# A threshold attention and FFN kernel: q and k transposed by TensorE instead of DMA, loads moved to SyncE, scores copied for the ACT path, weights loaded in pieces

## The chip, the cores and the metric

The kernel runs on one core of one Trainium2 chip. A core has five engines with a queue each, which run independently and wait for one another on semaphores: TensorE (PE; its weight loads are shown as PEld), VectorE (DVE), ScalarE (ACT), GpSimd (POOL) and SyncE (SP). SyncE computes nothing; it issues DMAs. DMAs issued by SyncE and by GpSimd run on the same 16 DMA engines. TensorE writes to PSUM, which DVE and ACT can read[...]; everything else is in SBUF.

The metric is the time of one execution on the device in microseconds, lower is better. Durations of single instructions come from one profiled execution.

## The reference

Eight batches of eight heads, 576 positions, head width 64. Attention keeps only the scores that lie within tau = 0.02 of their row's maximum:

```python
scores = scale * np.matmul(q, k.transpose(0, 1, 3, 2))        # scale = 1/8
thresh = np.max(scores, axis=-1, keepdims=True) - tau
scores = np.where(scores >= thresh, scores, -1000000000.0)
attn = np.exp(scores - np.max(scores, axis=-1, keepdims=True))
attn = attn / (np.sum(attn, axis=-1, keepdims=True) + 1e-09)
out = np.matmul(attn, v)
```

The attention output becomes x, of 4608 tokens by 512, and goes through a multiplicative FFN with d_ff = 1024:

```python
h = ((x @ w1) * (x @ w2)) @ w3
y = h @ w_out
```

Inputs and outputs are float32.

## The kernel before

**Pairs and units.** The work is cut into 32 pairs of heads (B = 8 batches, NP = 4 pairs each). A head's 576 rows are 512 main rows and 64 tail rows. The four main chunks of 128 rows of each of the two heads, and one chunk of the two tails together, give nine units (`UN`, L144). For a unit, `scores` (L147) multiplies q by k into a PSUM tile `S` of 128 x 576 floats; there are three such tiles.

**Precision.** A float32 value is carried as two bf16 numbers, a high part and the remainder. `hl` holds both side by side, 64 columns each, so that a transposed q chunk has the high parts on partitions 0 to 63 and the remainders on 64 to 127. Each score block takes two matmuls: against `kT`, and against `kB`, which is `kT` with its two partition halves swapped. So all four products of high parts and remainders are summed.

**Preparation.** `load_half` (L104) loads q, k and v of four heads, that is two pairs, with 13 DMAs that GpSimd issues. `prep_pair` (L123) then, for k and for q: DVE casts to the high part (L133), GpSimd subtracts for the remainder (L134), and SyncE issues a DMA transpose of the 128 x 1152 tile (L136). Two more SyncE DMAs build `kB` (L139, L140). ACT casts v (L127). The loop calls `load_half` two halves ahead and `prep_pair` two pairs ahead of use.

**Masking.** In `probs` (L174) a DVE pass over S finds the row's maximum less the margin (L188, the output `junk` is not used). Then a unit goes one of two ways, by the letter in `PATH` (L145). With A, ACT computes a leaky step from S (Prelu, L192) and an exponential of it with the row sum (L194). With P, ACT computes the exponential of S (L198) and DVE multiplies it by the mask and sums (L199). There are five P units and four A units per pair. The result `pm` of the two heads' chunks, 128 x 1152 bf16, is transposed by a DMA that SyncE issues (L203, four per pair; L206 for the tail unit). There are three `pm` tiles.

**Attention output.** `attend` (L210) takes the reciprocals of the row sums (L216), splits them on GpSimd (L218, L219), transposes them on PE (L224), spreads them over partitions with small matmuls (L230, L234), multiplies the transposed probabilities by v (L247, L259), and scales (L249, L260).

**FFN and the merged weight.** `merge_weights` multiplies w3 by w_out once into `wcb`, from DMA transposes of w3 (L90). `ffn` (L263) computes a batch's two products with w1 and w2 (L270), their product (L278), and the product with `wcb` (L286). `load_weights` issues four DMAs from GpSimd that cast to bf16 (L79 to L84).

**Order.** The main loop (L335) walks over 288 units. Generators on the `background` list are advanced by 0.72 steps per unit: first the weight loads, then the merge, then the FFN of finished batches. `attend` of a pair is written out as a block five units after the pair's last unit. The program order sets priorities; the framework's scheduler sets the final order within each engine's queue, and each queue runs in that order. Tiles with the same tag share their buffers, and a new tile waits until all uses of the one that it replaces have ended.

## Time and profile before

| | us |
|---|---|
| median of 3 runs | 683.06 (678.42 to 693.83) |
| the profiled execution | 677.28 |
| its span, first to last instruction | 675.3 |
| PE busy | 501.0 (74%) |
| PE weight loads busy | 260.1 (39%) |
| DVE busy | 456.4 (68%) |
| ACT busy | 388.0 (57%) |
| POOL busy | 241.0 (36%) |

The page of a profile gives busy times, the span in 40 equal slices with a digit for the busy tenths, the DMA queues with their packets and share of the 16 engines, the chain of work that ended last, the costliest groups of instructions, and the DMA issues. A group's line reads: source line, engine, operation, output <- inputs, shapes, count | busy us, mean ns of one | idle us of the engine before it, and what ended that idle time. A wait's line reads: who waited for whom, us in total, times, longest. A stretch's line gives for each engine its busy us and instructions, then the granted TensorE clock (1.00 is full), the DMA share and GB/s; a share can pass 1 because a packet's time includes its waiting. SPq is SyncE's queue. Matmuls overlap, so a busy PE is not PE at its peak.

### The profile page before, as it was taken

The page shows a single profiled execution, that of the slowest core. Times are in us where ns is not written, and L with a number is a line of the kernel's source. Part 1 is how long each engine was busy: PE and PEld are TensorE (multiplying, and loading weights), DVE is VectorE, ACT ScalarE, POOL GpSimd, SP SyncE. Part 2 cuts the span into 40 slices and gives each one's busy share as a digit, 9 for nine tenths or more (in the row PEclk, how much of TensorE's full clock was granted, in tenths as well). Part 3 has the DMA queues.
Part 4 walks back from the last instruction along what each step waited for, and adds up shares of the span by engine and source line. Part 5 has one row for each costly group of instructions (what it writes and reads, how often), then busy time and mean ns, then how long its engine had stood idle before and what let it go on. Part 6 is the DMA issues. An engine that isn't in the chain of part 4 may idle for free.

```text
span 675.3 us, 10319 instructions
## 1 busy us (share of the span) xinstructions
PE 501.0 (74%) x3163; PEld 260.1 (39%) x3208; DVE 456.4 (68%) x1181; ACT 388.0 (57%) x766; POOL 241.0 (36%) x378
## 2 busy tenths in 40 slices
PE   0530176658867888798878879888878888888996
PEld 0310042324434444344444435444434444444443
DVE  2630372259967898777968978798868988884231
ACT  1420162357756777566757766776766777774332
POOL 9870413513434344444343445344531120000000
PEclk9999988959979999777997979798998998999998
DMA  6999989889898999997899999999999988745011
GB/s 151 207 179 205 245 164 177 147 175 202 180 169 195 234 208 197 204 232 177 174 189 238 171 190 211 239 172 212 218 187 167 154 154 197 114 81 125 13 43 71
DMA packets 278566, 117.61 MB, mean 174 GB/s; under 512 B 261872, under 2 KB 262896, under 8 KB 277488
## 3 DMA queue, kind: packets, MB, share of 16 engines
q1 hardware_dynamic: 264112, 82.87, 67.7%
q0 software_dynamic: 14400, 34.09, 21.3%
q8 instruction: 25, 0.41, 0.3%
q14 instruction: 29, 0.24, 0.1%
HBM read 39.32 MB, written 9.44 MB: 72 GB/s over the span
## 4 chain that ended last, share of the span: by engine, by line
PE 42%; DMA 20%; DVE 12%; ACT 10%; issue 9%; POOL 4%; SPq 2%; DVEq 0%; POOLq 0%; ACTq 0%
PE ab L270 13%; PE S L157 9%; DMA pT<-pm 9%; PE av L247 7%; DVE junk L188 7%; PE yp L286 5%; DMA qT<-qhl 4%; ACT y L192 4%; PE S L162 2%; DMA kT<-khl 2%; DMA qf<-in_q_dram 2%; ACT pm L194 2%; DMA w3t<-w_223 2%; ACT bc L232 2%; PE tl L259 2%
## 5 line engine op out<-in xcount | busy, mean ns | idle before, releaser
L188 DVE TENSOR_SCALAR_CACHE_REDUCE junk<-S 128x576 bf16<-128x576 f32 x288 | 217.1, 754 | 33.0 <-PE S L157 17.3
L157 PE MATMUL S<-kT,qT 128*128 128x288 bf16 x512 | 148.3, 310 | 116.0 <-ACT y L192 60.3
L157 PEld LDWEIGHTS <-qT 128*128 128x128 bf16 x1024 | 99.6, 103 | 193.1 <-issue 94.8
L157 PE MATMUL S<-kB,qT 128*128 128x288 bf16 x512 | 148.1, 310 | 10.4 <-DMA kB<-kT 10.4
L192 ACT ACTIVATE y<-S,thr 128x576 bf16<-128x576 f32 x128 | 95.0, 742 | 99.3 <-DVE junk L188 97.7
L199 DVE SCALAR_TENSOR_TENSOR pm<-S,thr,e 128x576 bf16<-128x576 f32 x128 | 104.1, 813 | 42.2 <-DMA pT<-pm 41.7
L198 ACT ACTIVATE e<-S 128x576 f32<-128x576 f32 x160 | 102.7, 643 | 47.3 <-DVE junk L188 46.7
L194 ACT ACTIVATE pm<-y 128x576 bf16<-128x576 bf16 x128 | 87.2, 682 | 19.1 <-DMA pT<-pm 16.4
L134 POOL TENSOR_TENSOR khl<-kf,khl 128x576 bf16<-128x576 f32 x32 | 41.0, 1281 | 130.7 <-DVE khl L133 130.7
L278 DVE TENSOR_TENSOR ab<-ah,ab 128x512 bf16<-128x512 bf16 (+2 forms) x80 | 50.6, 633 | 52.3 <-PE ab L270 48.6
L275 ACT ACTIVATE ah<-ab 128x512 bf16<-128x512 f32 (+2 forms) x80 | 44.1, 552 | 51.0 <-PE ab L270 49.8
L286 PE MATMUL yp<-wcb,ab 128*128 128x512 bf16 (+1 forms) x280 | 71.9, 386 | 0.7 <-issue 0.2
L247 PE MATMUL av<-pT,vb 128*64 128x512 bf16 (+1 forms) x320 | 54.7, 458 | 20.1 <-ACT bc L232 13.0
L270 PE MATMUL ab<-xm,w2b 128*128 128x512 bf16 x250 | 66.6, 384 | 0.7 <-DVE ab L278 0.4
L270 PE MATMUL ab<-xm,w1b 128*128 128x512 bf16 x235 | 64.3, 380 | 0.8
L218 POOL CAST rhl<-rcp 128x9 bf16<-128x9 f32 x32 | 6.2, 193 | 161.0 <-DVE rcp L216 144.2
L133 DVE CAST khl<-kf 128x576 bf16<-128x576 f32 x32 | 23.8, 747 | 50.6 <-DMA kT<-khl 38.6
L134 POOL TENSOR_TENSOR qhl<-qf,qhl 128x576 bf16<-128x576 f32 x32 | 41.0, 1282 | 19.0 <-DVE qhl L133 18.7
L270 PEld LDWEIGHTS <-w2b 128*128 128x128 bf16 x320 | 29.0, 98 | 33.7 <-issue 11.7
L247 PEld LDWEIGHTS <-vb 128*64 128x64 bf16 (+1 forms) x320 | 21.1, 119 | 48.2 <-issue 42.6
L270 PEld LDWEIGHTS <-w1b 128*128 128x128 bf16 x320 | 28.4, 98 | 28.6 <-issue 2.7
L286 PEld LDWEIGHTS <-ab 128*128 128x128 bf16 (+1 forms) x296 | 28.0, 100 | 28.3 <-issue 1.8
(158 smaller groups left out, 625.4 us busy)
## 6 DMA issues: line engine op xcount, KB each, us to landing
kB<-kT SPq DMA_DIRECT2D x64, 144.0 KB, 2.7
kf<-in_k_dram POOLq DMA_DIRECT2D x32, 256.0 KB, 4.3
qf<-in_q_dram POOLq DMA_DIRECT2D x32, 256.0 KB, 5.4
vf<-in_v_dram POOLq DMA_DIRECT2D x32, 256.0 KB, 4.1
out_dram<-ys SPq DMA_DIRECT2D x8, 1024.0 KB, 5.1
pT<-pm SPq DMA_TRANSPOSE x128, 4.0
w_223<-in_moe_w_dram POOLq DMA_DIRECT2D x1, 2048.0 KB, 26.5
kf<-in_k_dram POOLq DMA_DIRECT2D x32, 32.0 KB, 4.3
```

Of the source, the lines that this page charges most:

```text
L134: nc.gpsimd.tensor_tensor(hl[:, :, 1, :], src[nm], hl[:, :, 0, :], ALU.subtract)
L157: nc.tensor.matmul(sp[:, half, 0:HB], lhsT=t["qT"][:, q0:q0 + 128], rhs=kk[w][:, c0:c0 + HB], start=(w == 0), stop=(w == 1))
L188: nc.vector.tensor_scalar(junk[:, :, :], sp, margin, -3e38, ALU.subtract, ALU.max, accum_out=thr[:, :])
L192: nc.scalar.activation(y[:, :, :], sp, AF.Prelu, scale=-1.0, bias=thr[:, :], alpha=0.125 / CUT)
L194: nc.scalar.activation(dst, y[:, :, :].rearrange("p a b -> p (a b)"), AF.Exp, scale=-CUT, accum_out=rs)
L198: nc.scalar.activation(e[:, :, :], sp, AF.Exp, scale=0.125)
L199: nc.vector.scalar_tensor_tensor(out=dst.rearrange("p (a b) -> p a b", a=2), in0=sp, scalar=thr[:, :], in1=e[:, :, :], op0=ALU.is_ge, op1= ...
L247: nc.tensor.matmul(av[o, :], lhsT=vb[kp, sl, :], rhs=pT[kp, :, sl, :], start=(g == 0), stop=(g == 4))
L270: nc.tensor.matmul(p[:, 0:nt], lhsT=w[:, c, f * 128:(f + 1) * 128], rhs=x(c), start=(c == 0), stop=(c == 3))
L275: nc.scalar.activation(ah[:, 0:nt], p[:, 0:nt], AF.Copy)
L278: nc.vector.tensor_tensor(ab[:, 0:nt], ah[:, 0:nt], ps[1][:, 0:nt], ALU.mult)
L286: nc.tensor.matmul(yp[0:c1 - c0, :], lhsT=abs_[f][:, c0:c1], rhs=wcb[:, f, :], start=(f == 0), stop=(f == NF - 1))
```

## The change

* q, k and v of four heads are loaded with one DMA each for the main rows, in runs of 1 KB, plus one each for the tail rows and one more for v. SyncE issues them, no longer GpSimd.
* The split of q and k into high part and remainder is done by GpSimd alone, and the cast of v too. Tails are split once per half, in `load_half`.
* TensorE transposes q and k, ten 128-column or 64-column pieces each, into a PSUM tile with the tag of the score tiles, and DVE copies it to SBUF. `kB` is built by two SyncE DMAs as before.
* `prep_pair` is now a generator with three steps, and runs one pair ahead: the split at unit 0, k's transposes at unit 5, q's at unit 7.
* In A units the DVE pass over S also writes the scores to SBUF, a small DVE instruction subtracts the margin from the maximum, and ACT's Prelu reads the SBUF copy. The tail unit becomes an A unit: four P and five A.
* `attend` is spread over the units of the next pair, a step at a time.
* The weights come in nine DMAs instead of four, one per background step, in program order on GpSimd's queue; w_out before w3.

```diff
--- before.py
+++ after.py
@@ -76,13 +76,21 @@
     wl = {}
 
     def load_weights():
-        nc.gpsimd.dma_start(w1b[:, :, :], moe_w1.rearrange("(c p) f -> p c f", p=128))
-        nc.gpsimd.dma_start(w2b[:, :, :], moe_w2.rearrange("(c p) f -> p c f", p=128))
+        def load(dst, src):
+            tc.keep_in_program_order(nc.gpsimd.dma_start(dst, src.rearrange("(c p) f -> p c f", p=128)))
+
+        for c in range(0, 4, 2):
+            load(w1b[:, c:c + 2, :], moe_w1[c * 128:(c + 2) * 128, :])
+            yield
+            load(w2b[:, c:c + 2, :], moe_w2[c * 128:(c + 2) * 128, :])
+            yield
         wl["w3"] = stage.tile([128, NF, d_ff], BF16, tag="w3", name="w3", bufs=1)
         wl["wo"] = stage.tile([128, NF, d_model], BF16, tag="wo", name="wo", bufs=1)
-        nc.gpsimd.dma_start(wl["w3"][:, :, :], moe_w3.rearrange("(c p) f -> p c f", p=128))
-        nc.gpsimd.dma_start(wl["wo"][:, :, :], moe_w_out.rearrange("(c p) f -> p c f", p=128))
-        yield
+        load(wl["wo"][:, :, :], moe_w_out)
+        yield
+        for c in range(0, NF, 2):
+            load(wl["w3"][:, c:c + 2, :], moe_w3[c * 128:(c + 2) * 128, :])
+            yield
 
     def merge_weights():
         for f in range(NF):
@@ -96,9 +104,7 @@
             yield
 
 
-
     pairs = {}
-
     halves = {}
 
     def load_half(m):
@@ -106,43 +112,66 @@
         b, h0 = divmod(4 * m, H)
         t = {}
         for nm, src in (("k", k), ("q", q), ("v", v)):
-            x = stage.tile([128, 2, 9, D], FP32, tag=nm + "f", name=nm + "f", bufs=2)
+            x = stage.tile([128, 4, 4, D], FP32, tag=nm + "f", name=nm + "f", bufs=2)
+            nc.sync.dma_start(
+                x[:, :, :, :].rearrange("p h j d -> p h (j d)"),
+                src[b, h0:h0 + 4, 0:M, :].rearrange("h (p j) d -> p h (j d)", j=4))
+            tails = src[b, h0:h0 + 4, M:S, :].rearrange("h r d -> r h d")
+
+            y = stage.tile([128 if nm == "v" else 64, 4, D], FP32, tag=nm + "t", name=nm + "t", bufs=2)
+            nc.sync.dma_start(y[0:64, :, :], tails)
+            if nm == "v":
+                nc.sync.dma_start(y[64:128, 0:2, :], tails[:, 1::2, :])
+            t[nm], t[nm + "t"] = x, y
+        for nm in ("k", "q"):
+            hl = stage.tile([64, 4, 2, D], BF16, tag=nm + "hlt", name=nm + "hlt", bufs=2)
+            nc.gpsimd.tensor_copy(hl[:, :, 0, :], t[nm + "t"][:, :, :])
+            nc.gpsimd.tensor_tensor(hl[:, :, 1, :], t[nm + "t"][:, :, :], hl[:, :, 0, :], ALU.subtract)
+            t[nm + "hlt"] = hl
+        vbt = stage.tile([128, 4, D], BF16, tag="vbt", name="vbt", bufs=3)
+        nc.gpsimd.tensor_copy(vbt[0:64, :, :], t["vt"][0:64, :, :])
+        nc.gpsimd.tensor_copy(vbt[64:128, 0:2, :], t["vt"][64:128, 0:2, :])
+        t["vbt"] = vbt
+        halves[m] = t
+
+    def prep_pair(n):
+
+        h = halves[n // 2]
+        h0 = 2 * (n % 2)
+        t = {"vbt": h["vbt"][0:64, h0:h0 + 2], "vbu": h["vbt"][64:128, n % 2]}
+        vb = stage.tile([128, 2, 4, D], BF16, tag="vb", name="vb", bufs=3)
+        nc.gpsimd.tensor_copy(vb[:, :, :, :], h["v"][:, h0:h0 + 2])
+        t["vb"] = vb
+        hls = {}
+        for nm in ("k", "q"):
+            hls[nm] = hl = stage.tile([128, 2, 4, 2, D], BF16, tag=nm + "hl", name=nm + "hl", bufs=2)
             for hh in range(2):
-                nc.gpsimd.dma_start(
-                    x[:, :, 5 * hh:5 * hh + 4, :].rearrange("p a j d -> p a (j d)"),
-                    src[b, h0 + hh:h0 + 4:2, 0:M, :].rearrange("h (p j) d -> p h (j d)", j=4))
-                nc.gpsimd.dma_start(
-                    x[64 * hh:64 * hh + 64, :, 4, :],
-                    src[b, h0 + hh:h0 + 4:2, M:S, :].rearrange("h r d -> r h d"))
-            t[nm] = x
-        x = stage.tile([64, 2, D], FP32, tag="v2f", name="v2f", bufs=2)
-        nc.gpsimd.dma_start(x[:, :, :], v[b, h0 + 1:h0 + 4:2, M:S, :].rearrange("h r d -> r h d"))
-        t["v2"] = x
-        halves[m] = t
-
-    def prep_pair(n):
-        src = {nm: x[:, n % 2] for nm, x in halves[n // 2].items()}
-        t = {}
-        vb = stage.tile([128, 9, D], BF16, tag="vb", name="vb", bufs=4)
-        nc.scalar.activation(vb[:, :, :], src["v"], AF.Copy)
-        vb2 = stage.tile([64, D], BF16, tag="vb2", name="vb2", bufs=4)
-        nc.gpsimd.tensor_copy(vb2[:, :], src["v2"])
-        t["vb"], t["vb2"] = vb, vb2
+                src = h[nm][:, h0 + hh, :, :]
+                nc.gpsimd.tensor_copy(hl[:, hh, :, 0, :], src)
+                nc.gpsimd.tensor_tensor(hl[:, hh, :, 1, :], src, hl[:, hh, :, 0, :], ALU.subtract)
+        pairs[n] = t
+        yield
         for nm in ("k", "q"):
-            hl = stage.tile([128, 9, 2, D], BF16, tag=nm + "hl", name=nm + "hl", bufs=2)
-            nc.vector.tensor_copy(hl[:, :, 0, :], src[nm])
-            nc.gpsimd.tensor_tensor(hl[:, :, 1, :], src[nm], hl[:, :, 0, :], ALU.subtract)
-            st = stage.tile([128, 9, 128], BF16, tag=nm + "T", name=nm + "T", bufs=3)
-            nc.sync.dma_start_transpose(st[:, :, :], hl[:, :, :, :].rearrange("p a b c -> p (a b c)"))
-            t[nm + "T"] = st[:, :, :].rearrange("p a b -> p (a b)")
-        kB = stage.tile([128, 9 * 128], BF16, tag="kB", name="kB", bufs=3)
-        nc.sync.dma_start(kB[0:64, :], t["kT"][64:128, :])
-        nc.sync.dma_start(kB[64:128, :], t["kT"][0:64, :])
-        t["kB"] = kB
-        pairs[n] = t
+            hl = hls[nm]
+            tp = psum.tile([128, 2048], BF16, tag="S", name="tp", bufs=3)
+            for hh in range(2):
+                nc.tensor.transpose(tp[:, M + hh * R:M + (hh + 1) * R], h[nm + "hlt"][:, h0 + hh, :, :],
+                                    ident[0:64, 0:64])
+                for j in range(4):
+                    c0 = hh * (M + 2 * R) + j * 128
+                    nc.tensor.transpose(tp[:, c0:c0 + 128], hl[:, hh, j, :, :], ident[:, :])
+            st = stage.tile([128, 2 * S], BF16, tag=nm + "T", name=nm + "T", bufs=2)
+            nc.vector.tensor_copy(st[:, :], tp[:, 0:2 * S])
+            t[nm + "T"] = st
+            if nm == "k":
+                kB = stage.tile([128, 2 * S], BF16, tag="kB", name="kB", bufs=2)
+                nc.sync.dma_start(kB[0:64, :], t["kT"][64:128, :])
+                nc.sync.dma_start(kB[64:128, :], t["kT"][0:64, :])
+                t["kB"] = kB
+            yield
 
     UN = [(hh, i) for i in range(4) for hh in range(2)] + [(2, 4)]
-    PATH = "PAPAPAPAP"
+    PATH = "PAPAPAPAA"
 
     def scores(n, u):
         t = pairs[n]
@@ -184,17 +213,22 @@
         dst = t["pm"][:, hh, :] if hh < 2 else pms[n % 2][:, 0:S]
         rs = t["rs"][:, u:u + 1]
         thr = work.tile([128, 1], FP32, tag="thr", name="thr", bufs=4)
-        junk = work.tile([128, 2, HB], BF16, tag="junk", name="junk", bufs=1)
-        nc.vector.tensor_scalar(junk[:, :, :], sp, margin, -3e38, ALU.subtract, ALU.max,
-                                accum_out=thr[:, :])
         if PATH[u] == "A":
-            y = work.tile([128, 2, HB], BF16, tag="y", name="y", bufs=2)
-            nc.scalar.activation(y[:, :, :], sp, AF.Prelu, scale=-1.0, bias=thr[:, :],
+
+            sc = work.tile([128, S], FP32, tag="sc", name="sc", bufs=3)
+            nc.vector.tensor_scalar(sc[:, :].rearrange("p (a b) -> p a b", a=2), sp, 1.0, -3e38,
+                                    ALU.mult, ALU.max, accum_out=thr[:, :])
+            y = work.tile([128, S], BF16, tag="y", name="y", bufs=2)
+            thm = work.tile([128, 1], FP32, tag="thm", name="thm", bufs=4)
+            nc.vector.tensor_scalar(thm[:, :], thr[:, :], margin, None, ALU.subtract)
+            nc.scalar.activation(y[:, :], sc[:, :], AF.Prelu, scale=-1.0, bias=thm[:, :],
                                  alpha=0.125 / CUT)
-            nc.scalar.activation(dst, y[:, :, :].rearrange("p a b -> p (a b)"), AF.Exp,
-                                 scale=-CUT, accum_out=rs)
+            nc.scalar.activation(dst, y[:, :], AF.Exp, scale=-CUT, accum_out=rs)
         else:
-            e = work.tile([128, 2, HB], FP32, tag="e", name="e", bufs=3)
+            junk = work.tile([128, 2, HB], BF16, tag="junk", name="junk", bufs=1)
+            nc.vector.tensor_scalar(junk[:, :, :], sp, margin, -3e38, ALU.subtract, ALU.max,
+                                    accum_out=thr[:, :])
+            e = work.tile([128, 2, HB], FP32, tag="e", name="e", bufs=2)
             nc.scalar.activation(e[:, :, :], sp, AF.Exp, scale=0.125)
             nc.vector.scalar_tensor_tensor(
                 out=dst.rearrange("p (a b) -> p a b", a=2), in0=sp, scalar=thr[:, :],
@@ -235,27 +269,25 @@
                              rhs=rTs[:, 64 * hh:64 * hh + 64], start=(hh == 0), stop=(hh == 1))
         nc.scalar.activation(bc[:, M:S], tl[:, 64:128], AF.Copy)
         yield
-        vb, vb2, pT, pTm = t["vb"], t["vb2"], t["pT"], t["pTm"]
+        vb, vbt, vbu, pT, pTm = t["vb"], t["vbt"], t["vbu"], t["pT"], t["pTm"]
         av = psum.tile([128, 512], FP32, tag="m", name="av")
         for g in range(5):
             for hh in range(2):
                 o = slice(64 * hh, 64 * hh + 64)
                 if g < 4:
-                    kp, sl = slice(0, 128), g + 5 * hh
+                    lhsT, rhs = vb[:, hh, g, :], pT[:, :, g + 5 * hh, :]
                 else:
-                    kp, sl = o, 4
-                nc.tensor.matmul(av[o, :], lhsT=vb[kp, sl, :], rhs=pT[kp, :, sl, :],
-                                 start=(g == 0), stop=(g == 4))
+                    lhsT, rhs = (vbu if hh else vbt[:, 0, :]), pT[o, :, 4, :]
+                nc.tensor.matmul(av[o, :], lhsT=lhsT, rhs=rhs, start=(g == 0), stop=(g == 4))
         nc.vector.tensor_tensor(xms[b][:, hp, :], av[:, :], bc[:, 0:M], ALU.mult)
         yield
         for g in range(5):
             for hh in range(2):
                 o = slice(64 * hh, 64 * hh + 64)
                 if g < 4:
-                    lhsT, rhs = vb[:, g + 5 * hh, :], pTm[:, g, o]
+                    lhsT, rhs = vb[:, hh, g, :], pTm[:, g, o]
                 else:
-                    lhsT = vb2[:, :] if hh else vb[0:64, 4, :]
-                    rhs = pTm[0:64, 4, o]
+                    lhsT, rhs = vbt[:, hh, :], pTm[0:64, 4, o]
                 nc.tensor.matmul(tl[o, 0:64], lhsT=lhsT, rhs=rhs, start=(g == 0), stop=(g == 4))
         nc.vector.tensor_tensor(xt[:, hp, b, :], tl[:, 0:64], bc[:, M:S], ALU.mult)
         yield
@@ -324,35 +356,43 @@
                 return
 
     load_half(0)
-    prep_pair(0)
+    for _ in prep_pair(0):
+        pass
     load_half(1)
-    prep_pair(1)
     background.append(load_weights())
     background.append(merge_weights())
     total = NPAIR * NU
-    LAG = 5
     credit = 0.0
-    for t in range(total + LAG):
+    running = []
+    prep = None
+    for t in range(total + NU):
         n, u = divmod(t, NU)
         if t < total:
             if u == 0 and n % 2 == 0 and n + 4 < NPAIR:
                 load_half(n // 2 + 2)
-            if u == 1 and n + 2 < NPAIR:
-                prep_pair(n + 2)
+            if u == 0 and n + 1 < NPAIR:
+                prep = prep_pair(n + 1)
+            if u in (0, 5, 7) and n + 1 < NPAIR:
+                next(prep)
             scores(n, u)
             probs(n, u)
-        d = t - LAG
-        if d >= 0 and d % NU == NU - 1:
-            m = d // NU
-            for _ in attend(m):
-                pass
-            if m % NP == NP - 1:
-                background.append(ffn_main(m // NP))
-                if m // NP == B - 2:
-                    background.append(ffn_tail(0, B - 1))
+        if running:
+            try:
+                next(running[0])
+            except StopIteration:
+                running.pop(0)
+                m = n - 1
+                if m % NP == NP - 1:
+                    background.append(ffn_main(m // NP))
+                    if m // NP == B - 2:
+                        background.append(ffn_tail(0, B - 1))
+        if u == 1 and n > 0:
+            running.append(attend(n - 1))
+            next(running[0])
         credit += 0.72
         step(int(credit))
         credit -= int(credit)
+    assert not running
     background.append(ffn_tail(B - 1, B))
     while background:
         step(1)
```

## The prediction

> **What bounds the kernel now.** I read the page's busy slices and DMA queues first, then the busy times by stretch, then landing times and waits, then single groups. From the page, one digit per fortieth of the span:
>
> ```profile
> PE   0530176658867888798878879888878888888996
> DVE  2630372259967898777968978798868988884231
> DMA  6999989889898999997899999999999988745011
> ...
> q1 hardware_dynamic: 264112, 82.87, 67.7%
> q0 software_dynamic: 14400, 34.09, 21.3%
> ```
>
> The DMA row is full from the second slice to about slice 33, whereas PE and DVE have holes in slices 3 to 8. q1 (SyncE's queue) is nearly all transposes. The stretches, each row giving busy us of PE, PEld, DVE, ACT, POOL, then granted clock, DMA share, GB/s:
>
> ```profile
> 0.00:21.60 21.60, 0.90 (x3) 0.28 (x3) 5.25 (x18) 2.54 (x3) 19.86 (x34) 1.00 0.72 181
> 47.00:80.00 33.00, 2.96 (x12) 1.39 (x10) 2.52 (x8) 3.57 (x7) 8.56 (x15) 1.00 1.14 219
> 80.00:143.00 63.00, 36.76 (x198) 18.12 (x200) 28.66 (x71) 23.86 (x45) 24.75 (x34) 0.83 0.99 176
> 143.00:509.00 366.00, 304.20 (x1985) 160.94 (x2013) 301.69 (x783) 251.70 (x499) 156.11 (x244) 0.92 1.01 198
> 509.00:615.00 106.00, 93.55 (x633) 49.49 (x642) 90.44 (x240) 78.65 (x157) 11.26 (x24) 0.97 0.75 140
> 615.00:675.30 60.30, 50.05 (x284) 23.23 (x287) 13.52 (x30) 16.89 (x35) 0.40 (x2) 0.97 0.21 60
> ```
>
> The reciprocal, one per head pair, marks progress: the first of the 32 starts at 47.1, the third at 143.3, the 25th at 509.0, the last at 615.1. So the kernel has four stages: 143.3 us for three pairs (start-up with weights), then 22 pairs at 16.6 us with loads, 7 at 15.2 us without, and 60 us of FFN remainder. In the third stage DVE has 13.7 us of work per pair, PE 13.8 and the DMA engines 1.01 x 16.6 = 16.8: DMA is the bound. In the fourth DMA is at 0.75 and the pace is still 15.2, 1.13 times PE's 13.4: that is the pace of the chain between engines. The start-up hole is DMA too. Landing times (last number, us) in 47 to 80, and the waits over the whole span (us, times, longest):
>
> ```profile
> kT<-khl SPq DMA_TRANSPOSE x1, 25.9
> qT<-qhl SPq DMA_TRANSPOSE x1, 21.3
> pT<-pm SPq DMA_TRANSPOSE x1, 10.5
> ```
>
> ```profile
> DVE pm L199 <- DMA pT<-pm: 41.7, 17, 5.8
> DVE khl L133 <- DMA kT<-khl: 38.6, 7, 24.3
> ```
>
> A transpose that lands in 4 us elsewhere takes 20 to 26 beside the weights, and DVE's cast waits 24 us at the head of its queue for the k buffer.
>
> **The change, part by part.**
>
> ```profile
> L188 DVE TENSOR_SCALAR_CACHE_REDUCE junk<-S 128x576 bf16<-128x576 f32 x288 | 217.1, 754 | 33.0 <-PE S L157 17.3 <-PE S L170 11.0
> L134 POOL TENSOR_TENSOR khl<-kf,khl 128x576 bf16<-128x576 f32 x32 | 41.0, 1281 | 130.7 <-DVE khl L133 130.7
> L218 POOL CAST rhl<-rcp 128x9 bf16<-128x9 f32 x32 | 6.2, 193 | 161.0 <-DVE rcp L216 144.2 <-PE S L157 16.7
> L133 DVE CAST khl<-kf 128x576 bf16<-128x576 f32 x32 | 23.8, 747 | 50.6 <-DMA kT<-khl 38.6 <-DMA kf<-in_k_dram 11.9
> L226 DVE COPY rTs<-rT 18x128 bf16<-18x128 bf16 x32 | 6.6, 207 | 2.1 <-PE rT L224 1.7
> L230 PE MATMUL bm<-rTs,sel 18*128 18x128 bf16 x128 | 13.8, 232 | 1.0 <-DVE rTs L226 1.0
> ```
>
> *DMA.* 64 transposes of q and k go. Each moves 1152 rows of 256 B, so 73,728 packets. q1's mean is 0.677 x 675.3 x 16 / 264,112 = 27.7 ns on one engine, so 73,728 x 27.7 / 16 = 128 us, 4.0 per pair. The loads move the same bytes from the same 1 KB runs, now on q1. I take their DMA time as unchanged: 12.8 us per pair are left, below PE and DVE. On SP, two transpose issues of about 1.36 us per pair become 3.5 load issues; an SP plain DMA takes 0.46 to 0.62 us here, about 2 us: no change. What is new is order: a load that waits for its buffer (free once GpSimd has split the half's second pair) holds the four P transposes behind it on SP, and ACT and DVE wait for P's buffers. Free if GpSimd is on time, up to 3 us every second pair if not.
>
> *GpSimd.* The 13 load issues per half (0.60 to 0.73 us each, 4.4 us per pair) and two subtractions (2.56) leave. From rows L134 and L218, a subtraction costs about 187 + 1.9 ns per element; the small casts (193 ns at 9 elements, 240 at 64) give 185 + 0.85. Per pair: v 0.62, four casts of 256 at 0.40, four subtractions at 0.67, tails 1.4, reciprocal 0.4: 6.7 us against 7.1 now. Here a rule speaks against the change: the Trainium skill, GPSIMD Engine Reference, "Engine selection", keeps two-input elementwise work off GpSimd as about twice as slow as VectorE. The row agrees on the ratio (1281 ns, against 576 elements at DVE's one per ns). By the rule the split would cost; by this trace GpSimd is idle over half of a pair, so 6.7 us is hidden unless its latency counts. k is needed at unit 5 (8 us in), q at unit 7 (11 us).
>
> *PE.* 20 transposes per pair. Four 128-column matmuls with their loads at L230 take 0.39 us, about 0.055 each after the first; so 20 cost 1.3 us with two group starts. The other end is 232 ns each without overlap, 4.6 us. I take 1.3, as they are independent. PE goes to 15.0 us per pair at the same clock. I know no reason for a gain.
>
> *DVE.* Out: two casts of 747 ns. In: two PSUM copies of 1152 bf16. At one element per cycle as L133 shows (about 1 ns, 150 fixed) a copy is 1.35 us. But L226 copies 128 elements from PSUM in 207 ns, when 150 + 133 would be 283; two per cycle give 217. By that row 0.75 us, equal to the casts. The Trainium skill, VectorE: DVE Perf Modes, "The perf-mode tier table", caps copies with PSUM at 2x, so it permits the row's value and no better. The fifth masked-multiply pass goes to ACT (-0.81 us); five threshold subtractions on one column enter, at most 207 ns each as for L226, at least 0.08 as the accumulator read: +0.65. DVE stays at 13.6 (14.8 at 1x). The maximum pass itself, with fp32 output, I keep at 754: its input from PSUM already runs one element per cycle.
>
> *ACT.* Minus v's cast (0.68 us), plus a Prelu, an Exp and an accumulator read (0.74 + 0.68 + 0.19) for an Exp of 0.64: +0.3, at 11.4 of 16 hidden. Reading SBUF copies frees a score buffer about one Prelu earlier (waits "S for ACT y" are 60 us in all), but two of eleven allocations are now for transposes. I count these as zero.
>
> *Weights.* Nine pieces in program order behind background steps instead of four DMAs at once. The bytes stay: the four saturate the queues from 41 to 77 us. Between full engines every P transpose still crawls. The Trainium skill, DMA: Bandwidth & Descriptors, "Measured", wants 1 MiB per DMA; every piece reads at least 1 MB, so by the rule or by the rows piecing costs nothing. What the stage should gain: no q/k transposes stuck behind weights, and no DVE cast waiting for them. At the front, scores complete at 21.6 us now because k, its transpose and the swap copy are serial; PE transposes save about 6. Then DMA's own work to the third reciprocal is now 143 us at about 1.0; less five q/k preparations (5 x 4 = 20 us) and less the interference I place at another 20, I take 100; ends 85 (all hidden but weights 35, nine P sets and loads) and 128.
>
> *The end.* Nine more background steps, about 5 of which stay for the end at 0.9 us of PE less what the gaps take: +2, so 62.
>
> **Sum.** For the pace I have two ends: 15.2, the present chain without DMA pressure, and (13.4 + 1.3) x 1.13 = 16.6 if PE's extra work carries the same overhead. I take 15.8. Then 100 + 29 x 15.8 + 62 + 2 (677.28 profiled run minus 675.3 span) = 622 against 677.28. The median of three is 683.06, 0.85% above the profiled run: 627 on that scale. The 55 us are 43 from start-up and 14 from the pace, less 2.
>
> **Rivals.** (1) *A lesser gain: PE and 1x copies take DMA's place.* DVE 14.8, PE 15.0, pace 16.6, start-up 125: 125 + 481 + 62 + 2 = 670, about 676. For: PE granted 0.92 and already at 83%. Against: L226. Here "the change does not shorten the weights" ends too.
> (2) *Slower: preparation comes one pair ahead instead of two, and its chain is too long.* k's transposes at unit 5 (1.3 us), a DVE copy behind one or two passes (2.2), SP behind one or two P transposes (2.7), landing of the swap copy (2.7): 8.9 us, where four units of 1.7 give 6.8. PE's scores of the next pair stand at the head of its queue. With 2.1 us of that plus 1 us for loads holding SP: pace 18.9, 100 + 548 + 62 + 2 = 712, about 718. Break-even with 677 is a pace of 17.7. For: PE, DVE and SP are FIFOs, and each P transpose holds SP for over a microsecond. Against: FFN and attention steps can fill PE, and an engine's order can place the transposes earlier.
> (3) *More gain:* weights hidden (85) and pace 15.0: 584, about 589.
>
> **Chances.** Forecast 0.45 (605 to 650), rival 1 0.20, rival 2 0.23, rival 3 0.12. Within 2% (669 to 697) is about what this kernel's measurement can tell from no change. From rival 1 about half falls there, from rival 2 a small part: faster 0.66, same 0.14, slower 0.20. The range 595 to 710 leaves out most of rival 3 and the upper half of rival 2; the forecast's own range is 605 to 650.
>
> **What would show it.** q1 with some 75,000 fewer transposes' packets; PSUM copies near 0.75 us; third reciprocal near 100; pace near 15.8; GpSimd's subtractions near 0.67 us; no DVE wait for kT. It is wrong if scores wait for kB or qT in every pair, if SP sits on loads waiting for GpSimd, or if weights keep PE empty as long as now.

## The result, and the profile after

The changed kernel takes 655.78 us (median, 650.54 to 656.11) against 688.44 us (678.42 to 694.86) of the kernel before on the same chip: a ratio of 0.9615, interval 0.9516 to 0.9715. Medians take all executions; ratios leave out those more than 1.5% above the fastest of the same kernel. It is faster by 3.9%, where 8.2% were forecast; 655.78 lies outside the forecast's own 605 to 650. The profiled execution's span is 654.1 us against 675.3.

The reciprocal, one per pair, shows where the 21.2 us went:

| us | before | predicted | after |
|---|---|---|---|
| third reciprocal | 143.3 | 100 | 111.4 |
| mean of the 29 intervals after it (the pace) | 16.27 | 15.8 | 16.55 |
| third to 25th, per pair | 16.62 | | 16.81 |
| 25th to last, per pair | 15.16 | | 15.74 |
| last reciprocal to end | 60.2 | 62 | 62.6 |

So start-up gave 31.9 us, the pace took back 8.3 (29 x 0.285), and the end took 2.4.

Where the 8.3 us lie matters. The kernel before comes out of its start-up hole with two short intervals (11.2 and 13.7 us; 14.5 and 16.1 in the changed kernel), and its last seven are short too. These nine make 9.8 us of difference. In the twenty between, the 5th to the 25th reciprocal, the changed kernel is 1.5 us ahead (339.3 against 340.8). So in the middle of the loop the two run level.

The page of the changed kernel, one digit per fortieth of the span, then the two DMA queues:

```profile
PE   2502679789798989898998998998899998898995
DVE  1602447888778787878888887885779887982221
DMA  7999999887879678966988678977786567553101
...
q1 hardware_dynamic: 229040, 92.83, 70.6%
q0 software_dynamic: 3216, 5.24, 4.9%
```

The solid row of nines in DMA now ends after slice 7, and PE is at 8 or 9 through most of the loop. There is still a hole in PE, in slices 3 and 4. By stretches (busy us of PE, PEld, DVE, ACT, POOL, then granted clock, DMA share, GB/s):

```profile
26.00:52.00 26.00, 1.24 (x12) 0.85 (x13) 2.93 (x8) 4.83 (x10) 8.18 (x16) 0.56 1.22 177
52.00:111.40 59.40, 40.59 (x246) 20.71 (x249) 26.47 (x80) 25.14 (x52) 17.63 (x37) 0.76 1.12 181
111.40:481.00 369.60, 329.55 (x2424) 179.29 (x2461) 298.54 (x857) 256.12 (x525) 139.12 (x308) 0.96 0.81 166
481.00:591.50 110.50, 100.34 (x750) 54.25 (x762) 91.33 (x267) 80.96 (x168) 24.54 (x57) 1.00 0.62 120
```

In the loop (third row, 22 pairs) the DMA share fell from 1.01 to 0.81, which is 13.6 us per pair, and the pace did not follow. Per pair PE is busy 15.0 us, DVE 13.6, ACT 11.6 and POOL 6.3. Those four figures are the predicted ones within 0.4. The durations were close too; first three groups of the page, then DVE's groups between 111.4 and 591.5:

```profile
L233 DVE SCALAR_TENSOR_TENSOR pm<-S,thr,e 128x576 bf16<-128x576 f32 x128 | 103.7, 810 | 41.5 <-DMA pT<-pm 31.7
L150 POOL CAST khl<-kf 128x256 bf16<-128x256 f32 x64 | 24.0, 396 | 68.3 <-PE tp L162 68.2
L151 POOL TENSOR_TENSOR khl<-kf,khl 128x256 bf16<-128x256 f32 x64 | 41.8, 667 | 0.6
```

```profile
L219 DVE TENSOR_SCALAR_CACHE_REDUCE sc<-S 128x576 f32<-128x576 f32 x145 | 107.8, 747 | 13.2 <-PE S L186 9.5 <-PE S L199 3.4
L164 DVE COPY kT<-tp 128x1152 bf16<-128x1152 bf16 x28 | 21.1, 752 | 5.5 <-PE tp L162 5.3
L223 DVE TENSOR_SCALAR thm<-thr 128x1 f32<-128x1 f32 x145 | 21.2, 147 | 0.9
```

The PSUM copy takes 752 ns (0.75 us predicted), the split 396 and 667 ns (400 and 670), the score-copying maximum pass 747 (754). q1 lost 35,072 packets and not 75,000, since the loads came onto it. What the prediction had wrong is what sets the pace. DVE's waits between 270 and 540 us show what came in place of DMA, first in the kernel before, then in the changed one:

```profile
DVE pm L199 <- DMA pT<-pm: 20.3, 10, 5.8
DVE junk L188 <- PE S L170: 4.5, 6, 1.1
```

```profile
DVE junk L229 <- PE S L186: 7.7, 15, 1.0
DVE sc L219 <- PE S L186: 7.6, 14, 1.4
...
DVE qT L164 <- PE tp L162: 4.4, 6, 1.7
DVE kT L164 <- PE tp L162: 3.5, 8, 0.8
DVE pm L233 <- DMA pT<-pm: 1.2, 2, 0.7
```

The wait for DMA went, 20.3 to 1.2 us in some 16 pairs, and waits for PE's scores and transposes of about the same length came: 23.2 us in the lines shown, where the kernel before has 4.5.

Start-up, in landing times (last number, us, issues between 20 and 60) and waits (us, times, longest, between 20 and 111):

```profile
w_324<-in_moe_w_dram POOLq DMA_DIRECT2D x4, 512.0 KB, 15.7
kB<-kT SPq DMA_DIRECT2D x2, 144.0 KB, 13.4
pT<-pm SPq DMA_TRANSPOSE x4, 21.9
```

```profile
PEld L186 <- DMA kB<-kT: 35.1, 2, 33.0
DVE pm L233 <- DMA pT<-pm: 30.6, 3, 23.0
PE S L186 <- DVE pm L233: 24.6, 3, 23.7
```

GpSimd issues five of the nine weight pieces at 20 to 25 us, one after another, and the four of w3 at 33.8, 45.1 and 53.5: they collide with the P transposes as the four whole loads did. A P transpose lands in 22 us, SP stands behind it, `kB` is issued late, and PE's weight load waits 33 us for it. SP's queue (start, us):

```profile
25.50 20.80 SPq L237 DMA_TRANSPOSE pT<-pm  x2
46.40 0.54 SPq L168 DMA_DIRECT2D kB<-kT  x1
```

### The profile page after: what moved, and what is told of

Its sections match the earlier page's. It is cut to its first block, busy times and chain, and to the rows that moved or that the text cites. A ratio compares the mean times of both kernels' runs of the same rounds, so it can differ in the third digit from the quotient of the medians.

```text
span 654.1 us, 11488 instructions
## 1 busy us (share of the span) xinstructions
PE 536.2 (82%) x3790; PEld 286.1 (44%) x3848; DVE 444.1 (68%) x1277; ACT 390.2 (60%) x798; POOL 209.3 (32%) x463
## 4 chain that ended last, share of the span: by engine, by line
PE 53%; DMA 17%; DVE 13%; ACT 8%; issue 5%; POOL 2%; SPq 1%; DVEq 0%; POOLq 0%; ACTq 0%
PE ab L302 15%; PE S L186 10%; DMA pT<-pm 8%; PE yp L318 8%; PE av L281 6%; PE tp L162 5%; DMA kB<-kT 5%; DVE pm L233 3%; DVE sc L219 3%; DVE junk L229 3%; ACT y L224 3%; DMA w3t<-w_324 2%; PE tp L158 2%; PE wp L101 2%; PE tl L291 2%
## 5 line engine op out<-in xcount | busy, mean ns | idle before, releaser
L224 ACT ACTIVATE y<-sc,thm 128x576 bf16<-128x576 f32 x160 | 122.8, 770 | 61.6 <-DVE thm L223 61.1
L186 PE MATMUL S<-kB,qT 128*128 128x288 bf16 x512 | 138.8, 295 | 19.0 <-DMA kB<-kT 18.7
L219 DVE TENSOR_SCALAR_CACHE_REDUCE sc<-S 128x576 f32<-128x576 f32 x160 | 118.9, 748 | 15.2 <-PE S L186 11.5
L229 DVE TENSOR_SCALAR_CACHE_REDUCE junk<-S 128x576 bf16<-128x576 f32 x128 | 95.5, 746 | 31.7 <-PE S L186 31.1
L232 ACT ACTIVATE e<-S 128x576 f32<-128x576 f32 x128 | 81.9, 641 | 43.7 <-DVE junk L229 43.3
L150 POOL CAST khl<-kf 128x256 bf16<-128x256 f32 x64 | 24.0, 396 | 68.3 <-PE tp L162 68.2
L151 POOL TENSOR_TENSOR qhl<-qf,qhl 128x256 bf16<-128x256 f32 x64 | 41.9, 668 | 0.9
L151 POOL TENSOR_TENSOR khl<-kf,khl 128x256 bf16<-128x256 f32 x64 | 41.8, 667 | 0.6
L322 ACT ACTIVATE ys<-yp 128x512 f32<-128x512 f32 (+1 forms) x37 | 21.9, 592 | 31.3 <-PE yp L318 31.1
L281 PE MATMUL av<-pT,vb 128*64 128x512 bf16 x256 | 37.5, 416 | 2.6 <-DMA pT<-pm 2.0
```

What stands on the lines that cost most here:

```text
L151: nc.gpsimd.tensor_tensor(hl[:, hh, :, 1, :], src, hl[:, hh, :, 0, :], ALU.subtract)
L186: nc.tensor.matmul(sp[:, half, 0:HB], lhsT=t["qT"][:, q0:q0 + 128], rhs=kk[w][:, c0:c0 + HB], start=(w == 0), stop=(w == 1))
L219: nc.vector.tensor_scalar(sc[:, :].rearrange("p (a b) -> p a b", a=2), sp, 1.0, -3e38, ALU.mult, ALU.max, accum_out=thr[:, :])
L224: nc.scalar.activation(y[:, :], sc[:, :], AF.Prelu, scale=-1.0, bias=thm[:, :], alpha=0.125 / CUT)
L229: nc.vector.tensor_scalar(junk[:, :, :], sp, margin, -3e38, ALU.subtract, ALU.max, accum_out=thr[:, :])
L232: nc.scalar.activation(e[:, :, :], sp, AF.Exp, scale=0.125)
```

## The experiments

Times are medians beside the kernel before on the same chip, with the ratio where there is one; 655.78 and 0.9615 are the changed kernel's. By the chip, the kernel before has medians of 684.04 to 691.87 us. "Third" is the start of the third reciprocal; pace is taken as above, from one profiled execution. The four executions of the changed kernel spread over 5.6 us, which is 0.2 us per interval, so paces 0.1 apart are not told from equal ones.

### The engines' load, one at a time

*Copies of the transposed q and k on ACT.*

```diff
-            nc.vector.tensor_copy(st[:, :], tp[:, 0:2 * S])
+            nc.scalar.activation(st[:, :], tp[:, 0:2 * S], AF.Copy)
```

> The changed kernel with the two PSUM copies of kT and qT on ACT instead of DVE: DVE 1.35 us less per pair, ACT about 2.2 more. Theory DVE (the busiest of the two mask engines, 13.4 of 16.5): pace 15.2 to 15.5, 620 to 630. Theory PE: within 1.5% of 656. Theory hand-overs: between the two, or slower if ACT's queue is late with kT.

639.62 us, 0.9357 (0.9303 to 0.9411): third 100.4, pace 16.46, end 60.1. DVE falls by 1.2 us per pair, ACT rises by 1.9, and the pace moves by 0.09. 11 of the 16 us are start-up, where PE's weight loads wait 4.5 us for `kB` instead of 35.1; how moving the copies does that was not traced. It beats both kernels.

*Every transpose of q and k twice.*

```diff
-                    nc.tensor.transpose(tp[:, c0:c0 + 128], hl[:, hh, j, :, :], ident[:, :])
+                    for _ in range(2):
+                        nc.tensor.transpose(tp[:, c0:c0 + 128], hl[:, hh, j, :, :], ident[:, :])
```

(and the tails' likewise)

> The changed kernel with each PE transpose of q and k done twice into the same place: 20 more 128-column matmuls with weight loads per pair, about 1.1 us of PE. Theory PE: the pace rises by 1.1 to 1.3 us, 32 to 40 us in all: 688 to 696. Theory swap chain, or DVE: PE has 1.7 us of slack per pair, so less than a third of it shows: 656 to 668.

669.15 us, 0.9735 (0.9669 to 0.9802): third 118.0, pace 16.68. Twenty more transposes per pair cost 0.13 us of pace; of the 11 us between the profiled executions, 7 are start-up.

*One product instead of two,* with no swapped copy; the low-order products are left out.

```diff
-                for w in range(2):
+                for w in range(1):
```

> The changed kernel without kB and with one score matmul in place of two (leaves the two mixed products out): PE loses 18 matmuls of 288 columns per pair, some 2.2 us, against the run without kB, whose pace was 16.45 us per pair. Theory PE: pace 14.0 to 14.6. Theory that the hand-overs of scores between PE, DVE and ACT set the pace, with PE's own work hidden: pace 16.0 to 16.5, PE's idle time up by 2.

637.86 us (one run): third 99.7, pace 16.31. PE loses sixteen 288-column matmuls and the tails' five per pair, and the pace moves by 0.24, of which 0.14 against the run that only lacks the swapped copy (below). The loop's stretches of this run, and of the one with doubled transposes:

```profile
115.00:495.00 380.00, 323.87 (x2064) 155.40 (x2094) 304.80 (x883) 260.16 (x544) 147.41 (x325) 0.86 0.68 147
```

```profile
118.00:602.00 484.00, 451.38 (x3767) 259.32 (x3764) 386.33 (x1117) 332.99 (x690) 163.62 (x365) 0.99 0.76 153
```

With less to do, PE was granted 0.86 of its clock, with more 0.99. PE's busy time per pair thus moved by less than its work, 14.8 us to 13.8 and to 15.6 over the 29 intervals, and the two runs test PE less sharply than was planned. None of the three loads alone is the limit.

*No FFN for batches 0 to 5.*

```diff
-                    background.append(ffn_main(m // NP))
+                    if m // NP >= 6:
+                        background.append(ffn_main(m // NP))
```

> The changed kernel with the FFN of the first six batches left out (their main rows are not computed): PE loses 5.1 us per pair, DVE 1.4, ACT 1.5, and the PSUM tiles of tag m are shared with nothing but attention. Theory PE: pace 11 to 12 until the seventh batch, then DVE at 12.2 is in the way: 13 to 13.5. Theory hand-overs: 15 to 16. If the two shared PSUM tiles were what binds, also 13 to 13.5, and this run alone can't tell that from PE.

609.21 us (one run): third 112.8, 15.0 us per pair from there to the 27th, where the changed kernel has 16.8. Between 113 and 473 us PE is busy 284.90 of 360.00 us and DVE 291.04; in the changed kernel 320.60 and 290.56. Attention alone takes 15 us per pair with no engine full; the FFN adds 1.8. The theory of hand-overs had 15 to 16. Which hand-over it is was not separated.

### Rival 2: the order and the swapped copy

*No swapped copy,* both products with `kT`, so the cross products are computed wrongly.

```diff
-                nc.sync.dma_start(kB[0:64, :], t["kT"][64:128, :])
-                nc.sync.dma_start(kB[64:128, :], t["kT"][0:64, :])
...
-        kk = (t["kT"], t["kB"])
+        kk = (t["kT"], t["kT"])
```

> The changed kernel without the two SyncE copies that build kB: both score matmuls read kT (this leaves the two products of high part with remainder out of the scores, and the matmul count as it is). Theory PE: the pace of 16.55 us per pair is PE's work (14.8) with the overhead of its hand-overs, so only the visible waits for kB go, 10 us at most: 645 to 656. Theory swap chain: scores of the next pair wait for a kB that is issued late behind P transposes, and that sets the pace: pace 15.6 to 15.8, 625 to 635.

639.38 us, 0.9305 (0.9229 to 0.9381): third 99.9, pace 16.45. In the loop the chain that rival 2 named is worth 0.1 us. Its 33 us wait is a matter of start-up, and worth 11.5 us there, by the third reciprocal.

*Transposes of k and q two units earlier.*

```diff
-            if u in (0, 5, 7) and n + 1 < NPAIR:
+            if u in (0, 3, 5) and n + 1 < NPAIR:
```

> The changed kernel with k's transposes at unit 3 and q's at unit 5 (5 and 7 in the change). Theory swap chain: two units (3.5 us) more for kB to land, the waits for kB vanish: 630 to 645. Theory PE: within 1% of 656. If GpSimd's split is late for unit 3, slower, 660 to 680, with PE waiting for khl.

679.56 us, 0.9884 (0.9818 to 0.995): third 113.6, pace 17.20. Waits over the whole span:

```profile
PEld L258 <- POOL rhl L253: 42.4, 29, 3.1
PE rT L258 <- POOL rhl L253: 32.5, 24, 2.8
```

In the changed kernel the second of these is 11.3 us in all. Earlier is worse: splits of q and k then stand ahead of the reciprocal's split `rhl` on GpSimd, and PE waits for that. The 21 us more of this wait are about what the pace lost (19 us). So it was GpSimd's queue, not PE's, that the earlier preparation got in the way of.

### The score tiles

*The masking of before:* no score copies, the Prelu reads S, the tail unit is a P unit again (five P units).

```diff
-    PATH = "PAPAPAPAA"
+    PATH = "PAPAPAPAP"
...
-            nc.scalar.activation(y[:, :], sc[:, :], AF.Prelu, scale=-1.0, bias=thm[:, :],
+            nc.scalar.activation(y[:, :, :], sp, AF.Prelu, scale=-1.0, bias=thr[:, :],
```

> The changed kernel with the masking of the kernel before: ACT's Prelu reads S from PSUM, no SBUF copy, no threshold subtraction, the tail unit masked on DVE. DVE stays about level (minus 0.65, plus 0.81 us per pair), ACT loses 0.3. If holding a score tile through the Prelu costs nothing: 650 to 660. If the early release is what carries part of the gain: 670 to 685, with PE waits for the Prelu as in the kernel before.

678.93 us, 0.9926 (0.988 to 0.9972): third 110.4, pace 17.31. This is the key run. All other parts of the change together gain less than 1%: third reciprocal 33 us earlier, and 30 us lost in the 29 intervals after it, 1.04 on average. Of these 30 us, 12 lie in the first two intervals and 10 in the last seven, where the kernel before is quick; in the twenty between it is 0.4 each. The copies, with the tail unit's move to ACT, then bring 0.76 us per pair, 22 us, spread over the whole loop. PE's waits between 270 and 540 us, first without copies, then in the changed kernel:

```profile
PE S L186 <- ACT y L221: 6.7, 6, 2.2
PE S L186 <- DVE pms L228: 6.2, 6, 1.6
PE S L186 <- DMA kB<-kT: 6.0, 4, 2.2
PE tp L158 <- ACT y L221: 4.7, 5, 1.3
```

```profile
PE S L186 <- DVE pm L233: 5.4, 10, 0.8
PE S L186 <- DMA kB<-kT: 2.7, 4, 1.5
PE S L186 <- DVE sc L219: 2.6, 4, 0.8
...
PE tp L158 <- DVE sc L219: 1.4, 2, 0.8
PE tp L158 <- DVE pm L233: 1.0, 2, 0.8
```

A matmul into S or tp that waits for y, pms, pm or sc waits for a score tile to come free. In these lines they are 17.6 us without copies and 10.4 with them, in some 16 pairs: 0.45 of the 0.76 us. The rest is not in PE's direct waits, and what the tail unit's move has in it was not separated.

*Two more uses of a score tile per pair, and the same small work in the tile that is held anyway.* Behind each copy of a transposed tile:

```diff
+            ex = psum.tile([128, 2048], BF16, tag="S", name="ex", bufs=3)
+            nc.tensor.transpose(ex[:, 0:64], h[nm + "hlt"][:, h0, :, :], ident[0:64, 0:64])
+            exs = stage.tile([128, 64], BF16, tag="exs", name="exs", bufs=2)
+            nc.vector.tensor_copy(exs[:, :], ex[:, 0:64])
```

(the control writes `tp[:, 1152:1216]` instead of `ex`)

> The changed kernel with two more uses of a score tile per pair (13 instead of 11): beside each of the two transposed tiles a further tile of the same three is taken, gets one small transpose of 64 rows, and a copy of 64 columns frees it. Theory A, the rotation of the three score tiles has replaced DMA as the limit: without the two transposed tiles the late pace was 14.7 instead of 16.5 us, 0.9 per use, so up to 18.3 and some 45 us more; at least +0.4 per use, pace above 17.3, time above 675. Theory B, the load of PE, DVE and GpSimd together or the order of the queues sets the pace and the tiles do not: as the run with the same small work in a tile that is held anyway, pace up by at most 0.3, time below 666.

> Control: the same small transpose and the same small copy, two per pair, but in the tile that the transposes hold anyway, so no further use of a score tile. Adds about 0.25 us of PE, 0.4 us of DVE per pair. Both theories: pace up by 0.1 to 0.3, time 656 to 666. If it costs as much as the run with two more uses, the tiles do not matter.

675.71 us, 0.9899 (0.9826 to 0.9973) with the further uses; 653.61 us, 0.9573 (0.945 to 0.9696) with the same work in the held tile. The small work costs nothing that can be seen. Taking a further tile for it costs 22 us, 0.7 us per pair, 0.35 per use. Theory A is right in kind, that a use has a price; the 0.4 to 0.9 that it named per use are too high. That the tiles are the limit does not follow. The profiled execution of the first took 679.84 us, so no pace is read from it.

*No transposes after pair 0* (pair 0's `kT` and `qT` serve all, no swapped copy, nine uses left), and *no splits after pair 0* (transposes and copies stay, on pair 0's values).

```diff
+            if n > 0:
+                t[nm + "T"] = first[nm]
+                yield
+                continue
```

```diff
+            if n > 0:
+                hls[nm] = first[nm]
+                continue
```

> The run without kB, and besides with q and k of the first pair's transposes used for all pairs (31 pairs get the first pair's scores): no transposes on PE, no copies on DVE after the first pair, and nine instead of eleven uses of the three score tiles per pair. Less PE work alone moved the pace by 0.1 us (one product), less DVE work alone by 0.1 (copies on ACT). Theory score tiles: what the transposes cost is their share of the three tiles; pace 14.0 to 15.2, from 16.45. Theory no single resource: 16.0 to 16.4.

> Leaves out the splits of q and k into high part and remainder after pair 0: transposes, copies and the swap copies stay, and work on pair 0's split values, so GpSimd is nearly idle. It tells GpSimd's part of the 1.9 us per pair that went when splits, transposes and copies all went. Theory A: at most 0.4 of it, late pace 16.1 to 16.6. Theory B with GpSimd as the cause (late splits, or DVE slowed beside it): late pace 14.7 to 15.3.

621.70 and 650.70 us (one run each). In both the loads of q and k run ahead of use and are done by the 13th pair, so the 13th to 25th reciprocal is what counts: 14.69 us per pair without transposes, 16.70 without splits, 17.01 in the changed kernel (17.16 in the kernel before). Without transposes the ten pairs ahead of that took 19.0 us each: GpSimd did the splits of later pairs then (131.19 of 190.00 us busy from 87 us on), and PE waited 31.2 us for `rhl`. Over all 29 intervals that run's pace is 16.19. The stretches from 277 us, first without transposes, then without splits:

```profile
277.00:476.00 199.00, 181.30 (x1264) 94.87 (x1262) 166.14 (x505) 159.55 (x330) 17.26 (x53) 0.99 0.66 131
```

```profile
277.00:476.00 199.00, 184.12 (x1361) 100.11 (x1362) 162.99 (x468) 139.84 (x288) 28.28 (x71) 0.97 0.69 138
```

GpSimd is nearly idle in both (17.26 and 28.28 of 199.00), so its splits and the loads are worth 0.3 us, and 2.0 us per pair hang on the transposes and what belongs to them: PE's work, DVE's copies, two uses of tiles, the swapped copy.

*The transposes in the two smaller PSUM tiles* of the FFN and the attention output, one head each.

```diff
-            tp = psum.tile([128, 2048], BF16, tag="S", name="tp", bufs=3)
             for hh in range(2):
+                tp = psum.tile([128, 1024], BF16, tag="m", name="tp")
...
+                nc.vector.tensor_copy(st[:, hh * S:(hh + 1) * S], tp[:, 0:S])
```

> The changed kernel with the transposes of q and k in the two smaller PSUM tiles of the FFN and the attention output (one head each, so four tiles of 576 columns and four copies of about 0.45 us per pair) instead of two score tiles. Theory A: nine uses of score tiles are left, the pace falls towards 15.5 and the time to 625 to 640, unless the two smaller tiles, which have some 24 uses per pair already, become the limit. Theory B: no gain, 656 or up to 10 us more for the two additional copies.

672.01 us, 0.9834 (0.97 to 0.9969), pace 17.26. Moving them to the other pool is worse by some 16 us, with two more copies per pair in it. Which of the two costs it was not separated.

*Scores of all nine units copied;* and the same *with the transposed copies on ACT*.

```diff
-            e = work.tile([128, 2, HB], FP32, tag="e", name="e", bufs=2)
-            nc.scalar.activation(e[:, :, :], sp, AF.Exp, scale=0.125)
+            e = work.tile([128, S], FP32, tag="e", name="e", bufs=2)
+            nc.scalar.activation(e[:, :], sc[:, :], AF.Exp, scale=0.125)
...
-                out=dst.rearrange("p (a b) -> p a b", a=2), in0=sp, scalar=thr[:, :],
-                in1=e[:, :, :], op0=ALU.is_ge, op1=ALU.mult, accum_out=rs)
+                out=dst, in0=sc[:, :], scalar=thm[:, :],
+                in1=e[:, :], op0=ALU.is_ge, op1=ALU.mult, accum_out=rs)
```

> The changed kernel with the scores of all nine units copied to SBUF by the maximum pass (four score copies), so that the P units, too, hold their score tile only until that pass ends and not through the exponential (0.64 us) and the mask (0.81 us). DVE gets four threshold subtractions of 0.15 us per pair more. Theory A, the three score tiles' rotation sets the pace: copying in five units was worth 0.76 us per pair, so four more are worth up to 0.6, pace near 16.0, time 638 to 650. Theory B, the engines' work sets it: pace up by the 0.6 us of DVE at most, time 656 to 670.

> The same with the copies of the transposed q and k on ACT (that version alone took 639.6, pace 16.46, third reciprocal 100.4). DVE 12.6, ACT 13.7 us per pair. Theory A: pace near 15.9, time 622 to 635, faster than every version so far. Theory B: 640 to 652.

663.26 and 642.59 us, where the versions without these copies took 655.78 and 639.62; pace 16.74 and 16.54 (16.55 and 16.46). Theory A had expected a gain in both: it fails here. The groups of the first of them, DVE's between 111 and 591 us, then GpSimd's between 117 and 603:

```profile
L229 DVE SCALAR_TENSOR_TENSOR pm<-sc,thm,e 128x576 bf16<-128x576 f32 x113 | 100.6, 891 | 3.9 <-ACT e L228 3.6
L220 DVE TENSOR_SCALAR thm<-thr 128x1 f32<-128x1 f32 x255 | 34.8, 141 | 0.6
```

```profile
L151 POOL TENSOR_TENSOR qhl<-qf,qhl 128x256 bf16<-128x256 f32 x52 | 38.6, 757 | 0.6
...
L150 POOL CAST khl<-kf 128x256 bf16<-128x256 f32 x52 | 28.1, 552 | 52.5 <-PE tp L162 46.6 <-issue 5.8
```

PE's waits between 270 and 540 us of the same run:

```profile
PE rT L254 <- POOL rhl L249: 12.9, 14, 2.5
PE S L186 <- DMA kB<-kT: 8.1, 6, 2.2
PE tp L158 <- DVE sc L217: 1.0, 2, 0.8
PE S L186 <- DVE sc L217: 0.7, 2, 0.4
```

The waits for tiles are almost gone, 10.4 to 1.7 us. In their place stand `rhl` (5.8 in the changed kernel) and `kB` (2.7). The mask pass with both inputs in SBUF takes 891 ns instead of 810, GpSimd's cast of k 552 and that of q 422 instead of 396, its subtractions 699 and 757 instead of 667. Sorted by what runs beside it, the mask pass takes 813 ns while GpSimd is idle (63 passes) and 1024 while GpSimd is busy for over 90% of it (43); in the changed kernel, where the scores come from PSUM, it takes 812 and 810. The Trainium skill, GPSIMD Engine Reference, "Specifications", says that GpSimd shares its SBUF interfaces with VectorE and contends with VectorE instructions that have two SBUF inputs; these figures agree. By the rows, what the run gained at the tiles it lost to four thresholds (0.56 us per pair), a slower mask (0.32) and a slower GpSimd; that these make up the whole of it is not shown.

### Start-up

*The kernel before with weights in nine pieces.*

```diff
-        nc.gpsimd.dma_start(w1b[:, :, :], moe_w1.rearrange("(c p) f -> p c f", p=128))
+        for c in range(0, 4, 2):
+            load(w1b[:, c:c + 2, :], moe_w1[c * 128:(c + 2) * 128, :])
+            yield
```

(w2, w3 and w_out likewise, as in the change)

> The kernel before with the nine weight loads of the change and nothing else. If the earlier start of the weights and their pieces made the start-up shorter (third reciprocal from 143 to 111 us): 650 to 665. If it was the q and k transposes leaving the queue: 680 to 690, with the start-up hole as long as before.

686.59 us beside 686.78 of the kernel before, 0.9846 (0.9783 to 0.9909): third 109.1 instead of 143.3, but the fourth is at 149.5 (154.5 in the kernel before, 125.9 in the changed one). Pieces alone move the hole by one pair; the third reciprocal flatters this version. Counted from the fourth, the change still gains 29 us at start-up, 5 of them to be had by pieces alone.

*One piece every fourth unit,* and the merge after the last.

```diff
+        if t % 4 == 3 and weights is not None:
+            if next(weights, 0) == 0:
+                weights = None
+                background.append(merge_weights())
```

> The changed kernel with the same nine weight pieces one every four units, ending in the fifth pair, and the merge after them. Theory that the weights' collision with the P transposes is what makes the start-up 111 us: pieces of 3.7 us of DMA each, spread over 36 units, hide: third reciprocal at 75 to 90, later pairs level, 625 to 640. If GpSimd issues them at once all the same, because nothing in its queue waits: 650 to 660.

645.66 us, 0.953 (0.9373 to 0.9688): third 86.7, pace 16.99, end 63.5. Landing times for issues between 20 and 60:

```profile
kB<-kT SPq DMA_DIRECT2D x4, 144.0 KB, 3.4
pT<-pm SPq DMA_TRANSPOSE x7, 5.1
```

Without the burst the P transposes land in 5 us instead of 22, and the third reciprocal comes 25 us earlier: the burst makes most of the hole. But of the 25 us 13 are lost again in the pace. By the program's order the merge and the FFN are then done later, beside pairs that ran without them; that this is the reason is not shown.

*Four tiles for P instead of three,* and *all three together* (spaced pieces, four tiles, copies on ACT).

```diff
-            t["pm"] = work.tile([128, 2, S], BF16, tag="pm", name="pm", bufs=3)
+            t["pm"] = work.tile([128, 2, S], BF16, tag="pm", name="pm", bufs=4)
```

> The changed kernel with four pm tiles instead of three (and eleven ab tiles instead of twelve, to make room). A pm tile lives from its first write to its transpose's landing, by my estimate 10 to 11 us, and three of them turn over four times in 16.5 us. Theory pm tiles: pace 15.5 to 16, and the start-up shorter by up to 7, since two more units run before the weights stop the transposes: 620 to 640. Otherwise start-up alone: 648 to 656.

> Copies of kT and qT on ACT, weights spaced, four pm tiles, together. If their gains add: 605 to 625. If the copies on ACT and the spacing gain the same microseconds of start-up: 625 to 640.

649.74 us, 0.9596 (0.9481 to 0.9711), not to be told from the changed kernel; and 640.03 us, 0.9451 (0.938 to 0.9522), no better than the copies on ACT alone. The third reciprocal of the combination is at 80.7, the pace 17.03. Four versions with a third reciprocal anywhere between 80.7 and 100.4 have their last one at 574.7 to 579.4: a start-up gain beyond the first 11 us was not kept.

## Why the prediction was wrong

- **DMA's own work: right.** The DMA share fell by 3.2 us per pair in the loop (4.0 predicted).
- **GpSimd, PE, DVE and ACT: right within 0.4 us per pair.** 6.3, 15.0, 13.6 and 11.6; PE at a clock of 0.96, though, not the 0.92 of before. That GpSimd hides the split held: leaving it out brought 0.3 us. The row behind it agrees less with "about twice as slow" than was said: 1281 ns against the 747 of DVE's cast of the same size is 1.7.
- **The pace, "I have two ends: 15.2 ... and ... 16.6 ... I take 15.8": wrong, and the step that failed.** It measured 16.55, 22 us over the sum. First, 15.2 was not the present chain without DMA pressure. The stretch that it was read from held four of the seven pairs' k and q transposes; in the rest the preparation had run out. Second, "DMA is the bound" was taken to mean that the pace falls as DMA is relieved. Relieved by 3 us per pair, the middle of the loop stayed as it was: 17.16 us per pair before and 17.01 after from the 13th to the 25th reciprocal, 17.37 with the masking of before. DVE's wait for DMA went (20.3 to 1.2 us), and its waits for PE's scores and transposes took that place. What the loop would do without DMA pressure and without transposes on PE is open, as that was not run. That the value met the other end, 16.6, does not make that end's reason right: it put PE's overhead of 1.13 on 1.3 us of transposes, and as many transposes again cost 0.13 us.
- **The score tiles, "I count these as zero": right as a sum, by luck, and wrong in its parts.** Earlier release, with the tail unit's move, is worth 0.76 us per pair, two uses about 0.7. Each is 20 to 22 us of the kernel, as large as the whole gain between the profiled executions. Put at nothing together, they hid that the change minus its copies gains almost nothing.
- **What sets the pace now** is not settled. Transposes and what belongs to them are worth 2.0 us per pair. Shown of this are 0.7 (two uses of tiles, measured by adding, not by taking away), 0.13 (PE) and some 0.1 each for DVE's copies and the swapped copy; about 1 us remains. The 2.0 is read from the 13th to the 25th reciprocal. There the two copies are worth more, 0.5 (16.53 with the copies on ACT) and 0.25 (16.76 without the swapped copy), and half a us remains; single traces don't decide it. The tiles are one of several limits close together: freeing them further brings `rhl` and `kB` to the fore.
- **Weights, "the interference I place at another 20" and 100 in all: mis-sized.** The third reciprocal came at 111.4. "Nine pieces in program order behind background steps" did not spread the load enough: five went out within 5 us, the rest by 55. The sentence that every P transpose still crawls was right (22 us); that `kB` would queue behind it on SP at start-up was not in the sum; without `kB` the third reciprocal comes at 99.9, 11.5 us earlier, about what was missing. That pieces cost nothing was right; what they gain alone is not seen in the medians (686.59 beside 686.78).
- **The end, 62: right** (62.6), though the background steps are eight more, not nine.
- **Rival 2: its place is real, its price is not.** One wait of 33 us at start-up, worth 11.5, and 0.1 us per pair in the loop, where 3.1 were allowed. Rival 1 had the pace (16.6) without its cause: DVE's copies took 0.75 us and not 1.35, and DVE 13.6 us per pair, not 14.8.

The sum of 622 misses the profiled run by 34 us: 22 from the pace, 11 from start-up, 1 from the end.

## What to carry to other kernels

When a change moves work to another engine, count what its results are held in: here two more uses of a rotating PSUM tile cost 0.7 us per pair where the work in them was free. Releasing such a tile earlier pays until another limit is met: in five of nine units it went with 0.76 us per pair, in the other four with nothing. A stretch at the end of a kernel is no sample of the loop without one resource's pressure, unless all of the loop's other work is in it. Taking a wait away from one resource gains nothing if the next one is as long. Loads cut into pieces spread out only if something holds the pieces apart; and a gain at start-up counts once the last marker has moved, not the third.

## What the runs showed of the hardware

PE's granted clock went with how busy PE was in the loop: 0.83 without the FFN (PE busy 79% of the stretch), 0.86 with one product (85%), 0.96 in the changed kernel (89%), 0.99 with doubled transposes (93%); the kernel before, 0.92 at 83%, is off this line, and no run isolates the cause. With the clock went the matmuls: those of 128 x 288 against `kT` took 290 ns on average between 150 and 470 us in the changed kernel, 304 with one product and 316 without the FFN. So work taken from PE was partly given back.

VectorE and GpSimd slowed each other where all scores were copied to SBUF. The mask pass went from 813 to 1024 ns with GpSimd at work beside it. GpSimd's casts of 256 elements took 399 ns with no mask pass beside them, and 727 with one beside them for over half of their time; with the scores in PSUM, in the changed kernel, 396 either way.
